# The opening of a chunk-attention and channel-mix kernel in another written order, with the diagonal blocks on the scalar engine

## The chip, the cores and the metric

The kernel runs on one core of a Trainium2 chip. The metric is the device time of one execution, in microseconds. The engines of the core work side by side, each through a queue of its own in the order in which the program was written: TensorE (PE) multiplies, VectorE (DVE) and ScalarE (ACT) do arithmetic on tiles, GpSimd (POOL) does what little is left to it, and SyncE (SP) issues the DMA transfers. One engine waits for another by semaphores.

## The reference

```python
# q, k, v: (8, 8, 576, 64): batch, heads, tokens, head width; chunks of 64 tokens
scores = matmul(q_chunk, k_chunk.T) / sqrt(64)
attn = exp(scores - max(scores)); attn = attn / (sum(attn) + 1e-9)
x = matmul(attn, v_chunk)                       # heads side by side: (8, 576, 512)

x_prev = x shifted by one token, zero at the start of each batch entry
xk = mu_k * x + (1 - mu_k) * x_prev             # mu_k, mu_r: 512 numbers each
xr = mu_r * x + (1 - mu_r) * x_prev
k = relu(xk @ w_k)                              # 512 -> 1024, w_k in float64
out = sigmoid(xr @ w_r) * ((k * k) @ w_v)       # w_r 512 x 512, w_v 1024 x 512
```

The weights arrive as 8-byte floats and are read as pairs of 32-bit words. Each is turned into a high and a low part on the chip, and each product with a weight is made of three passes: high by high, high by low, low by high.

## The kernel before

The 4608 tokens are cut into 36 tiles of 128 and 18 groups of two tiles (numbers 0 to 17). For each tile t the steps have these names, with a step number behind the point:

- `nq`, `nk`: load q and k of tiles 0 to 5 as they lie (L162); `bq`, `bk`: load q and k of a whole group, from group 3 on, as 32 x 32 blocks, 16 or 32 DMAs each (L200); `v`: load v, four DMAs (L179).
- `T`: turn q and k of a tile, for tiles 0 to 5 by PE with copies to `qT` and `kT`, later by DVE. `S`: scores (S.0 on PE), maximum, subtraction, exponential on ACT (S.3), sum, division. `P`: P.0 turns the probabilities on PE, P.1 copies them, P.2 multiplies them with v on PE (`xps`), P.4 copies the result to `x`.
- `Mk`, `Mr`: the two mixtures. For tiles 0 to 3 PE makes them (L520) by products with 16 diagonal blocks of 128 x 128, which hold mu and 1 - mu; for later tiles DVE does (L532). Then follow a high part (ACT) and a low part (DVE).
- `K` g fp: a quarter of the product with `w_k` for group g (24 matmuls into `pk`), relu, square, high and low part (`kk`). `R` g tl: the product with `w_r` (12 matmuls into `pr`) and the sigmoid. `V`: the product with `w_v` (`pv`, 24 matmuls a tile) and the output.
- `sw..`, `cw..`, `hw..`: load a weight piece of 1 MB (L251), four operations on its words (two on ACT, L255 and L259, two on DVE, L262 and L268), high part and low part. There are ten pieces: `wr0`, `wr1`, `wk0` to `wk3`, `wv0` to `wv3`. `mu`: load mu_k and mu_r (L213, L214). `dg`: make the diagonal blocks (L485).

The program has two stretches. `START` is an order written out by hand for everything up to the end of groups 0 and 1, in which the weights are loaded and converted; a letter behind a colon names the engine of a step (A for ACT, D for DVE, G for POOL). `GROUP` is the order for each of the groups 2 to 17: K, R and V of the group among the attention of the next group's tiles. Each engine's queue gets its instructions in the order of these words, so that an instruction that waits holds all that stands behind it on its engine. All DMAs are issued by SP, also in that order.

Some buffers tie steps together: `v` has two buffers, so a load of v for tile t waits for P.2 of tile t - 2. The diagonal blocks lie in the buffer with the tag `st`, which `wv2` and after it `wv3` use too: `wv2` can be loaded when the last product with a diagonal block has been made, and `wv3` when `wv2` has been converted. Scores and turned probabilities share one buffer in PSUM, and `pk` and the turned q and k of the opening share two.

Of the kernel before, what the change touches and what calls it, by code (L numbers as in the profile page):

```python
# [24 lines left out]


START = """
W:14 Mk0.0:D nq0.0 nk0.0 nq1.0 T0.2 T0.3:A nk1.0 swr1.0 T0.0 T1.0 T0.1:D P0.3:D S0.0 mu.0
dg.0:G swr0.0 S0.1:D T1.1:A v0.0 T1.2 S0.2:D T1.3:A S1.0 S1.1:D S0.3:A cwr1.1:A S1.2:D S0.4:D
cwr1.0:A S1.3:A S0.5:D nk2.0 nq2.0 P0.0 S1.4:D cwr0.1:A nk3.0 P0.1:A cwr1.2:D P0.2 T2.0 T2.2  # L30
Mk3.0:D cwr0.0:A S1.5:D cwr0.2:D nq3.0 P1.0 swk2.0 T2.1:A P0.4:A T3.2 v1.0 cwr0.3:D Mr0.0
P1.1:A T2.3:A T3.3:A S2.0 cwr1.3:D Mr0.1:A T3.0 Mk0.1 nq4.0 P1.3:D nk4.0 S2.1:D S2.2:D hwr1.0:A
T3.1:A nk5.0 S3.0 hwr1.1:D S2.3:A S3.1:D S3.2:D Mk0.2:A P1.2 Mr0.2:D P1.4:A T4.2 T4.0 T4.3:A
swk0.0 hwr0.0:A v2.0 S2.4:D cwk2.0:A Mk0.3:D T5.2 nq5.0 Mr1.0 S2.5:D hwr0.1:D swk1.0 T4.1:A
Mr1.1:A cwk2.1:A P2.3:D Mr1.2:D cwk0.1:A Mk1.1 cwk2.2:D P2.0 S3.3:A T5.0 Mk1.2:A S3.4:D Mk1.3:D
P2.1:A cwk0.0:A bk3.0 R00.0 P2.2 cwk2.3:D R01.0 R00.1:A swk3.0 P2.4:A bq3.0 hwk2.0:D Mk2.0:D
swv0.0 hwk2.1:D T5.3:A Mr2.0 cwk0.2:D cwk1.0:A cwk0.3:D cwk1.1:A S3.5:D hwk0.0:A K02.0 cwk1.2:D
P3.0 hwk0.1:D R01.1:A cwk1.3:D T5.1:A hwk1.0:D P3.1:A hwk1.1:D cwk3.0:A Mk2.1 S4.0 cwk3.1:A
cwk3.2:D K02.1:A Mr2.1:A cwk3.3:D cwv0.1:A hwk3.0:A v3.0 S4.1:D K00.0 K00.1:A swv1.0 v4.0
Mr2.2:D K00.2:A K01.0 P3.2 hwk3.1:D bq4.0 S4.2:D P3.3:D cwv0.0:A S5.0 K00.3:D P3.4:A K03.0  # L40
cwv0.2:D Mk2.2:D Mk2.3:D Mk3.1 K02.2:A K02.3:D Mk3.2:D Mr3.0 cwv1.0:A S4.3:A Mk3.3:D S4.4:D
K01.1:A K01.2:A Mr3.1:A cwv0.3:D hwv0.0:A K03.1:A P4.3:D cwv1.1:A Mr3.2:D swv2.0 S5.1:D S5.2:D
cwv2.1:A K01.3:D hwv0.1:D R10.0 cwv2.0:A S4.5:D K10.0 K11.0 cwv1.2:D cwv2.2:D cwv2.3:D hwv2.0:D
S5.3:A hwv2.1:D P4.0 P4.1:A K10.1:A cwv1.3:D R11.0 R10.1:A S5.4:D K03.2:A R11.1:A hwv1.0:A
K12.0 P4.2 K03.3:D K10.2:A v5.0 V001.0 V001.1 P4.4:A hwv1.1:D swv3.0 Mk4.0:D V001.2 K10.3:D
Mk4.1:D K11.1:A cwv3.0:A K13.0 V001.3 cwv3.1:A V001.4 cwv3.2:D cwv3.3:D S5.5:D K11.2:A K12.1:A
T6.0:D Mk4.2:A P5.0 hwv3.0:A Mk1.0:D P5.1:A V001.5 v6.0 hwv3.1:D K11.3:D Mr4.0:D V001.6 V001.7
V001.8:D P5.3:D P5.2 K13.1:A V11.0 V11.1 K12.2:A P5.4:A K12.3:D V001.9:D Mk5.0:D V11.2 Mk4.3:D
V10.0 V10.1 T6.1:D Mk5.1:D T7.0:D V11.3 K13.2:A Mr4.1:A K13.3:D Mk5.2:D V11.4 V11.5 Mr4.2:D
V10.2 V10.3 Mr5.0:D V10.4 Mk5.3:D V11.6 T7.1:D V10.5 Mr5.1:D V11.7 V10.6 V10.7 Mr5.2:D V11.8:D  # L50
V10.8:D bk4.0 v7.0
"""
# [26 lines left out]
def tile_chunk_attention_channel_mix(  # L79
# [147 lines left out]
    def convert(nm, src, a, n, dst, ring):  # L230

        st = f"{ring}:{nm}"

        def words():
            return T[st].rearrange("p a (n w) -> p a n w", w=2)  # L240
# [4 lines left out]
        def high():
            return words()[:, :, :, 1]

        def f_load(_):
# [2 lines left out]
            nc.sync.dma_start(out=T[st], in_=src)  # L251
# [4 lines left out]

        def f_a(_):
            x = low().bitcast(U32)
            nc.scalar.activation(low(), x, AF.Copy, scale=0.875 * 2.0**-29, bias=0.5)  # L259

        def f_s(_):
            nc.vector.scalar_tensor_tensor(  # L262
                out=low(), in0=high(), scalar=3, in1=low(),
                op0=ALU.logical_shift_left, op1=ALU.bitwise_or,
            )
# [10 lines left out]
        def f_lo(e):
            engine[e].tensor_tensor(dst(1), low().bitcast(F32), dst(0).bitcast(F32), ALU.subtract)  # L277
# [196 lines left out]
    def make_diag():  # L474
        do.task = "dg"

        def fn(_):
            T["diag"] = tmp.tile([P, 4, NB, P], F32, tag="st", name="diag", bufs=1)
            for i, (nm, mu) in enumerate((("k", muk), ("r", mur))):
                rest = const.tile([P, NB], F32, name=f"rest{nm}")  # L480
                nc.gpsimd.tensor_scalar(rest, mu, -1.0, 1.0, ALU.mult, ALU.add)
                for n, col in enumerate((mu, rest)):
                    to = diag[nm, n] = T["diag"][:, 2 * i + n]
                    for cb in range(NB):
                        nc.gpsimd.tensor_scalar(  # L485
                            to[:, cb], ident, col[:, cb : cb + 1], None, ALU.mult
                        )
# [75 lines left out]
    def moe_k(g, fp):  # L563
        def f_mm(_):
            pk = T[f"pk{g}{fp}"] = ps_k.tile([P, 2, G], F32, tag="k", name=f"pk_{g}_{fp}")
            xk = T[f"xk{g}"]
            for e in range(2):
                f = 2 * fp + e
                n = 0
                for cb in range(NB):  # L570
                    for a, b in PASSES:
                        nc.tensor.matmul(  # L572
                            pk[:, e, :],
                            wk[a][:, cb, f * P : (f + 1) * P],
                            xk[b][:, cb, :],
                            start=(n == 0),
                            stop=(n == 3 * NB - 1),
                        )
                        n += 1

        def f_relu(e):
            r = T[f"r{g}{fp}"] = mo.tile([P, 2, G], F32, tag="relu", name=f"relu_{g}_{fp}")
            pk = T[f"pk{g}{fp}"]
            if e == "D":
                nc.vector.scalar_tensor_tensor(
                    out=r, in0=pk, scalar=0.0, in1=pk, op0=ALU.max, op1=ALU.mult
                )
                return
            nc.scalar.activation(r, pk, AF.Relu)  # L589
            nc.scalar.activation(r, r, AF.Square)  # L590
# [192 lines left out]
```

## Time and profile before

| what | value |
| --- | --- |
| median of 3 runs (lowest, highest) | 642.67 us (638.86, 645.74) |
| profiled execution, its own time | 639.14 us |
| its span from the first to the last instruction | 637.4 us |
| PE busy | 610.6 us, 96% |
| DVE busy, ACT busy, POOL busy | 400.0, 330.0, 14.7 us |
| mean granted clock of PE | 0.976 |
| DMA | 49.17 MB, mean 77 GB/s |

Busy shares are means over the span. The table of 40 slices (15.9 us each) tells the stages apart: slices 1 to 8 hold START, the rest the regular groups and the last group. In a view by time, a row begins with its start and its length; a number in brackets at its end is how long the engine stood idle before it and what ended that.

### The profile page before, as it was taken

What the parts mean: (1) busy time and instruction counts of PE and PEld (TensorE: products, weight loads), DVE (VectorE), ACT (ScalarE), POOL (GpSimd) and SP (SyncE); (2) the same over time, 40 slices, a digit from 0 to 9 for tenths busy, and PEclk for the clock granted to TensorE, in tenths of its full rate; (3) what the DMA queues carried; (4) which work ended last, traced back from release to release, by engine and by line L of the source; (5) the groups of instructions that cost most, each with busy time, mean ns of one, the idle gap of its engine ahead of it and who ended that gap; (6) DMA issues with size and microseconds to landing.
All of it is one profiled execution on the core that took longest, in us unless ns stands there. A gap on an engine that the chain in (4) does not pass through costs nothing.

```text
span 637.4 us, 14033 instructions
## 1 busy us (share of the span) xinstructions
PE 610.6 (96%) x5676; PEld 535.7 (84%) x5676; DVE 400.0 (63%) x859; ACT 330.0 (52%) x504; POOL 14.7 (2%) x24
## 2 busy tenths in 40 slices
PE   6779799989999999999999999999999999999997
PEld 5768787877989898979797979797979797979895
...
PEclk9789699997999999999999999999999999999999
...
GB/s 220 187 200 172 123 94 83 97 37 78 67 54 65 75 83 54 80 55 81 54 65 54 79 75 67 55 70 72 76 54 64 71 86 67 35 34 34 14 21 33
DMA packets 195072, 49.17 MB, mean 77 GB/s; under 512 B 186817, under 2 KB 186817, under 8 KB 195009
## 3 DMA queue, kind: packets, MB, share of 16 engines
...
q14 instruction: 20, 0.16, 0.1%
...
## 4 chain that ended last, share of the span: by engine, by line
PE 79%; SPq 8%; DMA 7%; POOL 2%; DVE 1%; issue 1%; ACT 1%; POOLq 0%; DVEq 0%; ACTq 0%
PE pv L647 30%; PE pk L572 27%; PE pr L617 14%; SPq L200 6%; DMA wv_st<-in_moe_w_v 3%; PE xps L435 3%; PE s L360 2%; DMA wk_st<-in_moe_w_k 2%; PE pt L417 2%; POOL diag L485 2%; SPq L162 1%; DMA muk<-in_moe_mu_k 1%; DMA k<-in_k 1%; SPq L179 1%; DVE wv_st L262 0%
## 5 line engine op out<-in xcount | busy, mean ns | idle before, releaser
L572 PE MATMUL pk<-xkhi,wk 128*128 128x256 f32 x1152 | 218.5, 286 | 1.6 <-ACT relu L589 1.6
L647 PE MATMUL pv<-wv,kk 128*128 128x512 f32 x864 | 205.4, 395 | 0.0
L647 PEld LDWEIGHTS pv<-wv,kk 128*128 128x128 f32 x864 | 161.6, 187 | 39.7 <-DVE wv L277 0.4
L572 PEld LDWEIGHTS pk<-xkhi,wk 128*128 128x128 f32 x1152 | 182.1, 190 | 4.0 <-ACT relu L589 2.0
L572 PE MATMUL pk<-xklo,wk 128*128 128x256 f32 x576 | 162.9, 283 | 0.0
L572 PEld LDWEIGHTS pk<-xklo,wk 128*128 128x128 f32 x576 | 109.7, 191 | 0.8
L589 ACT ACTIVATE relu<-pk 128x512 f32<-128x512 f32 x72 | 42.6, 592 | 106.3 <-PE pk L572 105.2
L617 PE MATMUL pr<-wr,xrhi 128*128 128x512 f32 x288 | 96.2, 415 | 0.0
L602 DVE TENSOR_TENSOR kk<-relu,kk 128x512 fp32r<-128x512 f32 x72 | 49.4, 687 | 68.3 <-ACT kk L131 68.3
L617 PEld LDWEIGHTS pr<-wr,xrhi 128*128 128x128 f32 x288 | 53.1, 194 | 11.7
L617 PE MATMUL pr<-wr,xrlo 128*128 128x512 f32 x144 | 58.1, 403 | 0.0
L370 DVE TENSOR_REDUCE m<-s 128x8 f32<-128x512 f32 x36 | 24.7, 687 | 53.0 <-PE s L360 53.0
L131 ACT ACTIVATE xrhi<-mixr 128x512 fp32r<-128x512 f32 x31 | 19.6, 632 | 55.8 <-DVE mixr L532 55.8
L131 ACT ACTIVATE xkhi<-mixk 128x512 fp32r<-128x512 f32 x31 | 19.6, 631 | 53.1 <-DVE mixk L532 53.1
L590 ACT ACTIVATE relu<-relu 128x512 f32<-128x512 f32 x72 | 45.5, 632 | 2.3
L131 ACT ACTIVATE kk<-relu 128x512 fp32r<-128x512 f32 x72 | 45.5, 632 | 2.1
L532 DVE SCALAR_TENSOR_TENSOR mixk<-d,muk,x 128x128 f32<-128x128 f32 (+1 forms) x144 | 38.5, 333 | 1.0
L532 DVE SCALAR_TENSOR_TENSOR mixr<-d,mur,x 128x128 f32<-128x128 f32 (+1 forms) x144 | 38.4, 331 | 0.0
L660 DVE TENSOR_TENSOR out<-pv,sg 128x512 f32<-128x512 f32 x36 | 24.0, 674 | 19.5 <-PE pv L647 18.6
L551 DVE TENSOR_TENSOR xrlo<-mixr,xrhi 128x512 fp32r<-128x512 f32 x32 | 22.2, 692 | 21.0 <-ACT xrhi L131 21.0
L551 DVE TENSOR_TENSOR xklo<-mixk,xkhi 128x512 fp32r<-128x512 f32 x32 | 22.1, 692 | 20.9 <-ACT xkhi L131 20.9
L435 PEld LDWEIGHTS xps<-pT,v 64*64 64x64 f32 x1152 | 21.1, 141 | 16.7 <-issue 8.9
...
## 6 DMA issues: line engine op xcount, KB each, us to landing
...
```

Of the source, the lines that this page charges most:

```text
L131: nc.scalar.activation(to, x, AF.Copy)
L200: nc.sync.dma_start(out=dst[pp : pp + 32, hp, s // 32 : (s + n) // 32, :], in_=src[b, j * HP + hp, t0 : t0 + n, dh * 32 : (dh + 1) * 32].r ...
L370: nc.vector.tensor_reduce(out=heads(m), in_=scores(), axis=AX.X, op=ALU.max)
L435: nc.tensor.matmul(T[f"xps{g}"][halves[c], 2 * j + a, tl * TT + e * CH : tl * TT + (e + 1) * CH], T[f"v{t}"][halves[j], hp, e, :], T[f"pT{ ...
L532: nc.vector.scalar_tensor_tensor(out=m[:, cb, s : s + w], in0=d[:, cb, s : s + w], scalar=mu[:, cb : cb + 1], in1=x[:, cb, c : c + w], op0 ...
L551: engine[e].tensor_tensor(lo[:, :, part], T[f"m{nm}{t}"], hi[:, :, part].bitcast(F32), ALU.subtract)
L572: nc.tensor.matmul(pk[:, e, :], wk[a][:, cb, f * P : (f + 1) * P], xk[b][:, cb, :], start=(n == 0), stop=(n == 3 * NB - 1),)
L589: nc.scalar.activation(r, pk, AF.Relu)
L590: nc.scalar.activation(r, r, AF.Square)
L602: engine[e].tensor_tensor(lo, T[f"r{g}{fp}"], hi.bitcast(F32), ALU.subtract)
L617: nc.tensor.matmul(pr, xr[a][:, cb, tl * TT : (tl + 1) * TT], wr[b][:, cb, :], start=(n == 0), stop=(n == 3 * NB - 1),)
L647: nc.tensor.matmul(T[f"pv{g}{tl}"], kk[a][:, f, tl * TT : (tl + 1) * TT], wv[b, f // 4][:, f % 4, :], start=(f == 0 and n == 0), stop=(f = ...
```

## The change

The change rewrites the order of START, puts the loads of mu into ACT's DMA queue, makes the diagonal blocks on ACT instead of POOL (the two small vectors 1 - mu on DVE), and cuts the relu step in two words, relu and square. The loader of a weight piece can now take ACT's queue as well; but no word of the new START asks it to, so all ten weight pieces are still issued by SP. The words of GROUP give the same instructions in the same order as before.

```diff
 START = """
-W:14 Mk0.0:D nq0.0 nk0.0 nq1.0 T0.2 T0.3:A nk1.0 swr1.0 T0.0 T1.0 T0.1:D P0.3:D S0.0 mu.0
-dg.0:G swr0.0 S0.1:D T1.1:A v0.0 T1.2 S0.2:D T1.3:A S1.0 S1.1:D S0.3:A cwr1.1:A S1.2:D S0.4:D
+W:14 Mk3.0:D nq0.0 nk0.0 T0.2 T0.0 T0.3:D mu.0:A T0.1:D Mk0.0:D nq1.0 P0.3:D nk1.0 T1.0 S0.0
+S0.1:D swr0.0 dg.0:A v0.0 S0.2:D nk2.0 S0.3:A T1.1:D T1.2 T1.3:A cwr0.0:A S1.0 nk3.0 cwr0.1:A
...
-Lq K0.0 Sa.0 Sb.0 Sa.12 K0.12 Sa.3 Sb.12 K0.3 Sb.3 Sa.45 Sb.45 K1 K2.0 Pa.0 K2.123 Pa.1
+Lq K0.0 Sa.0 Sb.0 Sa.12 K0.123 Sa.3 Sb.12 K0.4 Sb.3 Sa.45 Sb.45 K1 K2.0 Pa.0 K2.1234 Pa.1
...
+    def queue(e):
+        return nc.scalar if e == "A" else nc.sync
...
-            nc.sync.dma_start(out=muk, in_=mu_k.rearrange("(c p) -> p c", p=P))
+            queue(e).dma_start(out=muk, in_=mu_k.rearrange("(c p) -> p c", p=P))
...
-            nc.sync.dma_start(out=T[st], in_=src)
+            queue(e).dma_start(out=T[st], in_=src)
...
-                nc.gpsimd.tensor_scalar(rest, mu, -1.0, 1.0, ALU.mult, ALU.add)
+                nc.vector.tensor_scalar(rest, mu, -1.0, 1.0, ALU.mult, ALU.add)
...
-                        nc.gpsimd.tensor_scalar(
-                            to[:, cb], ident, col[:, cb : cb + 1], None, ALU.mult
-                        )
+                        if e == "A":
+                            nc.scalar.activation(
+                                to[:, cb], ident, AF.Copy, scale=col[:, cb : cb + 1]
+                            )
...
```

The first place is the head of ACT's queue. Before, it began with the copies of the turned q and k and the first exponential (`p_0`):

```order
L131 ACT_TABLE_LOAD
L131 ACTIVATE kT_106<-trk_0_131 128x4x128
L131 ACTIVATE qT_105<-trq_1_146 128x4x128
L131 ACTIVATE kT_106<-trk_1_204 128x4x128
L380 ACTIVATE p_0_209<-p_0_209 128x512
```

Now the same place holds the loads of mu and the 16 diagonal blocks:

```order
L216 DMA muk_99<-in_moe_mu_k 128x4x1
L217 DMA mur_100<-in_moe_mu_r 128x4x1
L489 ACT_TABLE_LOAD
L489 ACTIVATE diag_175<-ident_94,muk_99 128x128 x4
L489 ACTIVATE diag_175<-ident_94,restk_176 128x128 x4
L489 ACTIVATE diag_175<-ident_94,mur_100 128x128 x4
L489 ACTIVATE diag_175<-ident_94,restr_186 128x128 x4
L383 ACTIVATE p_0_201<-p_0_201 128x512
L131 ACTIVATE kT_106<-trk_1_208 128x4x128
```

Of the three copies, two (`kT` of tile 0 and `qT` of tile 1) have gone to DVE, the third stands behind the exponential, and the exponential stands behind the blocks.

The second place is SP's queue in the middle of START. Before, from the load of piece `wk1` on (`k_3` and `q_3` are the block loads `bk3` and `bq3`):

```order
L251 DMA wk1_st_467<-in_moe_w_k 128x4x512
L200 DMA k_3_506<-in_k 32x8x32 x16
L251 DMA wk3_st_569<-in_moe_w_k 128x4x512
L200 DMA q_3_572<-in_q 32x8x32 x16
L251 DMA wv0_st_590<-in_moe_w_v 128x2x1024
L179 DMA v_3_686<-in_v 64x4x64 x4
L251 DMA wv1_st_721<-in_moe_w_v 128x2x1024
L179 DMA v_4_723<-in_v 64x4x64 x4
L200 DMA q_4_774<-in_q 32x4x32 x32
L251 DMA wv2_st_904<-in_moe_w_v 128x2x1024
```

And now:

```order
L254 DMA wk1_st_426<-in_moe_w_k 128x4x512
L182 DMA v_2_452<-in_v 64x4x64 x4
L254 DMA wk3_st_466<-in_moe_w_k 128x4x512
L254 DMA wk2_st_485<-in_moe_w_k 128x4x512
L182 DMA v_3_608<-in_v 64x4x64 x4
L254 DMA wv1_st_693<-in_moe_w_v 128x2x1024
L254 DMA wv0_st_706<-in_moe_w_v 128x2x1024
L203 DMA q_3_747<-in_q 32x8x32 x16
L182 DMA v_4_811<-in_v 64x4x64 x4
L254 DMA wv2_st_826<-in_moe_w_v 128x2x1024
L182 DMA v_5_992<-in_v 64x4x64 x4
L203 DMA k_3_1012<-in_k 32x8x32 x16
```

`v_3` has moved ahead of both block loads of group 3, and the weights of `w_k` and two of `w_v` stand ahead of them too. `wk2`, the first of the `w_k` pieces before, is now the last.

The third place is the end of START in SP's queue. Before:

```order
L662 DMA out_0<-out_1_0_1313 128x512
L200 DMA k_4_1316<-in_k 32x4x32 x32
L179 DMA v_7_1349<-in_v 64x4x64 x4
L200 DMA q_5_1357<-in_q 32x8x32 x2
L179 DMA v_8_1618<-in_v 64x4x64 x4
```

And now:

```order
L674 DMA out_0<-out_0_0_1193 128x512
L182 DMA v_6_1215<-in_v 64x4x64 x4
L674 DMA out_0<-out_0_1_1225 128x512
L182 DMA v_7_1289<-in_v 64x4x64 x4
L203 DMA k_4_1314<-in_k 32x4x32 x32
L674 DMA out_0<-out_1_1_1348 128x512
```

`v_7` has moved from behind the 32 DMAs of `k_4` to ahead of them.

More of the change, by code (lines that the diff above doesn't have):

```diff
@@ L27 @@
 START = """
-W:14 Mk0.0:D nq0.0 nk0.0 nq1.0 T0.2 T0.3:A nk1.0 swr1.0 T0.0 T1.0 T0.1:D P0.3:D S0.0 mu.0
-dg.0:G swr0.0 S0.1:D T1.1:A v0.0 T1.2 S0.2:D T1.3:A S1.0 S1.1:D S0.3:A cwr1.1:A S1.2:D S0.4:D
[L30 to L51, printed above, removed]
+W:14 Mk3.0:D nq0.0 nk0.0 T0.2 T0.0 T0.3:D mu.0:A T0.1:D Mk0.0:D nq1.0 P0.3:D nk1.0 T1.0 S0.0
@@ new lines @@
+S0.1:D swr0.0 dg.0:A v0.0 S0.2:D nk2.0 S0.3:A T1.1:D T1.2 T1.3:A cwr0.0:A S1.0 nk3.0 cwr0.1:A
+S0.4:D S0.5:D S1.1:D T2.2 S1.2:D T2.3:A nq2.0 cwr0.2:D P0.0 cwr0.3:D P0.1:A P0.2 swr1.0 S1.3:A
+T3.2 P0.4:A nq3.0 S1.4:D S1.5:D hwr0.0:A cwr1.0:D Mr0.0 cwr1.1:A v1.0 T2.0 P1.0 swk0.0 hwr0.1:D
+nq4.0 T2.1:A P1.1:A P1.3:D cwr1.2:D Mk0.1 nk4.0 T3.3:A cwr1.3:D Mr0.1:A S2.0 T3.0 S2.1:D P1.2
+Mk0.2:A Mr0.2:D nq5.0 T3.1:A S2.2:D S3.0 P1.4:A nk5.0 T4.2 swk1.0 S3.1:D cwk0.1:A Mk0.3:D
+cwk0.0:A S3.2:D S2.3:A T4.0 T4.3:A Mk1.1 hwr1.0:A v2.0 Mr1.0 swk3.0 T4.1:A Mk1.2:A T5.2 Mr1.1:A
@@ new lines @@
+S2.4:D S2.5:D T5.3:A hwr1.1:D Mk1.3:D S3.3:A swk2.0 cwk0.2:D cwk0.3:D cwk1.1:A Mr1.2:D P2.0
+P2.1:A hwk0.0:A S3.4:D T5.0 S3.5:D P2.3:D Mk2.0:D Mk1.0:D hwk0.1:D R00.0 P2.2 R00.1:A R01.0
+P2.4:A cwk2.1:A cwk1.0:D cwk1.2:D T5.1:A P3.0 cwk1.3:D P3.1:A cwk2.0:A Mr2.0 Mr2.1:A K00.0
+hwk1.0:D v3.0 hwk1.1:D cwk2.2:D R01.1:A P3.2 cwk2.3:D cwk3.0:A S4.0 K01.0 S5.0 swv1.0 P3.3:D
+Mk2.1 swv0.0 cwk3.1:A hwk2.0:A cwk3.2:D hwk2.1:D cwk3.3:D K00.1:A K01.1:A K02.0 K00.2:A
+hwk3.0:D cwv0.0:A K01.2:A hwk3.1:D bq3.0 cwv0.1:A Mr2.2:D K03.0 P3.4:A cwv1.0:A Mk2.2:A
@@ new lines @@
+cwv0.2:D P4.3:D cwv0.3:D Mk3.1 Mk2.3:D v4.0 cwv1.1:A Mr3.0 swv2.0 Mk3.2:D Mk3.3:D S4.1:D
+K00.3:A Mr3.1:A K00.4:D hwv0.0:A Mr3.2:D K02.1:A R10.0 K10.0 K01.3:A T6.0:D K02.2:A cwv1.2:D
+K02.3:A K01.4:D cwv1.3:D R11.0 R10.1:A K03.1:A cwv2.0:A cwv2.1:A K11.0 hwv0.1:D K03.2:A K02.4:D
+R11.1:A K03.3:A S5.1:D cwv2.2:D V001.0 cwv2.3:D K10.1:A K03.4:D hwv2.0:A hwv1.0:A S4.2:D S4.3:A
+hwv2.1:D K12.0 V001.1 v5.0 hwv1.1:D V001.2 K10.2:A S5.2:D S4.4:D S5.3:A bk3.0 K11.1:A K11.2:A
+K10.3:A S4.5:D S5.4:D K10.4:D swv3.0 P4.0 P4.1:A K11.3:A S5.5:D cwv3.1:A V001.3 P4.2 cwv3.0:D
@@ L52 @@
+K11.4:D K12.1:A K13.0 K12.2:A bq4.0 P4.4:A V001.4 cwv3.2:D cwv3.3:D hwv3.0:A P5.3:D P5.0 V001.5
+T7.0:D P5.1:A K13.1:A hwv3.1:D V001.6 Mk4.0:D K12.3:A V001.7 Mk4.1:D V001.8:D Mk4.2:A P5.2 v6.0
+V10.0 P5.4:A V001.9:D V10.1 V11.0 Mk5.0:D Mr4.0:D V11.1 K13.2:A K13.3:A Mr4.1:A Mk4.3:D K12.4:D
+Mk5.1:D V10.2 V10.3 Mk5.2:A K13.4:D V11.2 V11.3 V10.4 Mr4.2:D Mk5.3:D V11.4 V10.5 V11.5 v7.0
+T6.1:D V10.6 Mr5.0:D Mr5.1:D V10.7 V11.6 Mr5.2:D V11.7 bk4.0 T7.1:D V11.8:D V10.8:D
 """
 GROUP = """
-Lq K0.0 Sa.0 Sb.0 Sa.12 K0.12 Sa.3 Sb.12 K0.3 Sb.3 Sa.45 Sb.45 K1 K2.0 Pa.0 K2.123 Pa.1
@@ L57 @@
-K3.0 Pb.0 Pb.1 K3.123 Tc R0 Pa.2 Pb.2 Pa.34 Pb.34 Lv Lk Mka R1 Mkb Mra Mrb Td V0 V1
+Lq K0.0 Sa.0 Sb.0 Sa.12 K0.123 Sa.3 Sb.12 K0.4 Sb.3 Sa.45 Sb.45 K1 K2.0 Pa.0 K2.1234 Pa.1
+K3.0 Pb.0 Pb.1 K3.1234 Tc R0 Pa.2 Pb.2 Pa.34 Pb.34 Lv Lk Mka R1 Mkb Mra Mrb Td V0 V1
 """
@@ L210, in load_mu, with fn @@
         do.task = "mu"
-        def fn(_):
-            nc.sync.dma_start(out=muk, in_=mu_k.rearrange("(c p) -> p c", p=P))
-            nc.sync.dma_start(out=mur, in_=mu_r.rearrange("(c p) -> p c", p=P))
+        def fn(e):
+            queue(e).dma_start(out=muk, in_=mu_k.rearrange("(c p) -> p c", p=P))
+            queue(e).dma_start(out=mur, in_=mu_r.rearrange("(c p) -> p c", p=P))
         do(fn, "Q")
@@ L246, in high, with f_load @@
             return words()[:, :, :, 1]
-        def f_load(_):
+        def f_load(e):
             pool_, bufs = dict(st=(tmp, 1), kk0=(mx, 2), kk1=(mx, 2)).get(ring, (wts, 1))
             T[st] = pool_.tile([P, a, 2 * n], I32, tag=ring, name=f"{nm}_st", bufs=bufs)
-            nc.sync.dma_start(out=T[st], in_=src)
+            queue(e).dma_start(out=T[st], in_=src)
         def f_y(_):
@@ L475, in make_diag, with fn @@
         do.task = "dg"
-        def fn(_):
+        def fn(e):
             T["diag"] = tmp.tile([P, 4, NB, P], F32, tag="st", name="diag", bufs=1)
@@ L484, in fn @@
                     for cb in range(NB):
-                        nc.gpsimd.tensor_scalar(
-                            to[:, cb], ident, col[:, cb : cb + 1], None, ALU.mult
-                        )
-        do(fn, "G")
+                        if e == "A":
+                            nc.scalar.activation(
+                                to[:, cb], ident, AF.Copy, scale=col[:, cb : cb + 1]
+                            )
+                        else:
+                            nc.vector.tensor_scalar(
+                                to[:, cb], ident, col[:, cb : cb + 1], None, ALU.mult
+                            )
+        do(fn, "D")
     def x_mix(t):
@@ L582, in f_relu, with f_sq @@
             r = T[f"r{g}{fp}"] = mo.tile([P, 2, G], F32, tag="relu", name=f"relu_{g}_{fp}")
-            pk = T[f"pk{g}{fp}"]
             if e == "D":
[L585 to L590, printed above, removed]
+                nc.vector.tensor_scalar(r, T[f"pk{g}{fp}"], 0.0, None, ALU.max)
+            else:
+                nc.scalar.activation(r, T[f"pk{g}{fp}"], AF.Relu)
+        def f_sq(e):
+            r = T[f"r{g}{fp}"]
+            if e == "D":
+                nc.vector.tensor_tensor(r, r, r, ALU.mult)
+            else:
+                nc.scalar.activation(r, r, AF.Square)
         def f_hi(e):
@@ L606, in moe_k @@
         do(f_relu, "A")
+        do(f_sq, "A")
         do(f_hi, "A")
```

## The prediction, made before the changed kernel had run

> **What bounds the kernel now.** I read the page's busy shares and its 40 slices first.
>
> ```profile
> PE 610.6 (96%) x5676; PEld 535.7 (84%) x5676; DVE 400.0 (63%) x859; ACT 330.0 (52%) x504; POOL 14.7 (2%) x24
> PE   6779799989999999999999999999999999999997
> PEclk9789699997999999999999999999999999999999
> GB/s 220 187 200 172 123 94 83 97 37 78 67 54 65 75 83 54 80 55 81 54 65 54 79 75 67 55 70 72 76 54 64 71 86 67 35 34 34 14 21 33
> ```
>
> PE bounds the whole, and from slice 11 on it is full at the full clock: nothing that the change touches can shorten that. In the first ten slices PE has gaps, and the clock falls there too. So I read the chain that ended last for the regular beat of a group.
>
> ```profile
> 194.24 2.84 PE pk L572 x24
> 197.07 1.09 PE s L360 x64
> 207.76 2.80 PE pr L617 x12
> 214.66 11.20 PE pv L647 x48
> 228.69 1.09 PE s L360 x64
> ```
>
> A group's scores follow the last ones after 228.69 - 197.07 = 31.62 us, all of it PE work: a K step is 2.84, an R step 2.80, the V of two tiles 11.20. Every gain must come from before that beat sets in. PE's timeline shows where the beat is broken first.
>
> ```profile
> 126.29 1.16 PE L360 MATMUL s<-kT,qT 64*64 64x64 f32 x64
> 143.80 0.44 PE L435 MATMUL xps<-pT,v 64*64 64x64 f32 x2 [3.30 <-DMA v<-in_v]
> 165.37 1.16 PE L360 MATMUL s<-kT,qT 64*64 64x64 f32 x64
> ```
>
> Group 2 started at 126.29 - 2.84 = 123.45 and took 165.37 - 126.29 = 39.08 us, 7.46 more than the beat. START took the rest, 123.45 us.
>
> **The change part by part.** Four losses of before should go, two new waits come. First the **wait for v of tile 7** in group 2, just shown: 3.30 us of idleness at its first load, and matmuls at a lowered clock behind it. So a wait costs its idleness and up to 4 us of lowered clock behind it. SP's timeline says why v was late.
>
> ```profile
> 124.78 16.46 SPq L200 DMA_DIRECT2D k<-in_k  x32
> 141.34 2.58 SPq L179 DMA_DIRECT2D v<-in_v  x4
> ```
>
> The 32 DMAs of k for group 4 take 16.46 us to issue, and v of tile 7 stood behind them. Now v stands ahead, so the loss of 7.46 goes. What is late next is that k: DVE turns it in the middle of group 2.
>
> ```profile
> 140.16 0.71 DVE L336 STREAM_TRANSPOSE qT<-q 128x512 f32<-128x512 f32 x1
> ```
>
> DVE needs it 140.16 - 123.45 = 16.7 us into the group. Its issue now begins after the stores of group 0 and two loads of v (2 x 2.58). Those stores come when V of group 1 (11.20) is still to do, so the issue begins some 6 us before group 2 and ends 16.5 later, 10.5 into it: 6 us of room. If that cover were gone, DVE would hold the mixtures of the next tiles behind it.
>
> Second, the **wait for v of tile 3** in START.
>
> ```profile
> 62.02 0.27 PE L572 MATMUL pk<-xkhi,wk 128*128 128x256 f32 x1
> 65.33 1.84 PE L435 MATMUL xps<-pT,v 64*64 64x64 f32 x32 [3.03 <-DMA v<-in_v]
> 69.02 1.13 PE L360 MATMUL s<-kT,qT 64*64 64x64 f32 x32 [1.86 <-DVE p L376]
> 75.36 1.95 PE L520 MATMUL mxk<-x,diag 128*128 128x128 f32 x16
> ```
>
> On SP's side of it:
>
> ```profile
> 38.69 9.32 SPq L200 DMA_DIRECT2D k<-in_k  x16
> 48.60 10.49 SPq L200 DMA_DIRECT2D q<-in_q  x16
> 59.68 2.58 SPq L179 DMA_DIRECT2D v<-in_v  x4
> ```
>
> From 62.29 to 75.36 lie 13.07 us with one `xps` and one scores step (1.09 for two tiles, so 0.55 each) and one K step: 3.94 of work, 9.1 lost. The load was issued at 59.68, behind 9.32 + 10.49 us of block loads. Now both stand behind it, and the 9.1 goes as far as nothing else holds PE there.
>
> Third, **POOL's diagonal blocks**.
>
> ```profile
> 23.15 0.63 PE L520 MATMUL mxr<-x,diag 128*128 128x128 f32 x2
> 24.89 2.23 PE L520 MATMUL mxr<-x,diag 128*128 128x128 f32 x14 [1.11 <-POOL diag L485]
> 27.05 0.69 PE L360 MATMUL s<-kT,qT 64*64 64x64 f32 x32
> ```
>
> The first mixture took 27.05 - 23.15 = 3.90 us; at full rate a mixture is 1.78 (75.36 to 77.14, the next mixture's start). 2.1 goes, since ACT has the blocks done by 14 (below).
>
> Fourth, a **load of `wk0` in ACT's way**.
>
> ```profile
> 37.32 0.60 PE L417 MATMUL pt<-ident,p 128*128 128x128 f32 x4
> 40.36 0.63 PE L315 MATMUL trq<-ident,qn 128*128 128x128 f32 x4 [2.44 <-ACT p L380]
> 45.27 0.69 PE L435 MATMUL xps<-pT,v 64*64 64x64 f32 x32
> 38.64 1.10 ACT L259 ACTIVATE wk_st<-wk_st 128x1024 int32<-128x1024 uint32 x1 [1.28 <-DMA wk_st<-in_moe_w_k]
> ```
>
> ACT stood before `wk0` until 38.64 with the exponential behind it, and PE waited. From 37.32 to 45.27 are 7.95 us for two turnings (0.43 each) and one R (2.80): 4.3 lost. Now `wk0` is issued ahead of tiles 4 and 5, so this wait goes.
>
> Of the new waits, the first is **ACT's blocks ahead of the first exponential**. DVE makes 1 - mu behind the first maximum, so 12 of the 16 blocks come after that.
>
> ```profile
> 9.75 0.69 DVE L370 TENSOR_REDUCE m<-s 128x8 f32<-128x512 f32 x1 [0.85 <-PE s L360]
> 11.21 0.63 ACT L380 ACTIVATE p<-p 128x512 f32<-128x512 f32 x1 [0.30 <-DVE p L376]
> ```
>
> For a block's price I read the groups by shape:
>
> ```profile
> L131 ACT ACTIVATE x<-xps 128x256 f32<-128x256 f32 x8 | 2.6, 394 | 0.0
> L131 ACT ACTIVATE wr<-wr_st 128x1024 fp32r<-128x1024 f32 x2 | 2.3, 1130 | 0.0
> L131 ACT ACTIVATE kT<-trk 128x512 f32<-128x512 f32 x6 | 3.5, 596 | 6.6 <-PE trk L315 6.6
> ```
>
> No row has 128 elements on ACT. Above, it is no dearer than 256 (394 ns); below, the slope from 512 to 1024 alone gives (1130 - 596)/4 = 134. Twelve take 1.6 to 4.7 us; I take 0.25 each, 3.0, since 256 is the nearest row and copies overlap a little. The exponential then starts near 10.4 + 0.4 + 3.0 = 13.8, not 11.21; behind it on ACT stand the copy of the turned k of tile 1 and the first weight steps, and DVE's sum and PE's second scores wait. DVE now does that sum at once, before tile 1's maximum, which gives 1 us back: **1.5** lost, between 0 and 3.
>
> The Trainium skill ("ScalarE: Activation LUTs", What ACT_TABLE_LOAD costs) gives 186 ns plus 0.833 a column, 93 more for a scale read per partition, and 93 of overlap. By it 512 columns are 613, as the 596 above agrees, but a block is an estimated 293 ns, and the loss would be 2.0 instead of 1.5.
>
> The second new wait is **`wk2` on ACT**. Its first step stands on ACT ahead of `wk1`'s second, of tile 5's turned q and of P.1 of tile 3; so DVE's part of `wk1`, the second K step, P.2 of tile 3 and the scores of tile 5 wait. From `wk2`'s landing to that K step there are two ACT steps and four on DVE.
>
> ```profile
> L262 DVE SCALAR_TENSOR_TENSOR wk_st<-wk_st 128x1024 int32<-128x1024 int32 x4 | 4.9, 1226 | 3.5 <-ACT wk_st L259 3.5
> L133 DVE CAST wk<-wk_st 128x1024 fp32r<-128x1024 f32 x2 | 1.4, 694 | 0.1
> ```
>
> How fast the pieces can come shows in a stretch of 4 us (the last two columns are the share of the DMA engines and GB/s):
>
> ```profile
> 32.00:36.00 4.00, 3.19 (x30) 2.99 (x29) 3.93 (x8) 3.43 (x5) 0.00 (x0) 1.00 0.97 287
> ```
>
> From landing to K step these are 2 x 1.1 (the 1130 above) + 3 x 1.2 + 0.7 = 6.5 us. Up to `wk2` there are 10.2 MB to load (two wr and four wk pieces, q and k of six tiles, v of three). At the 200 GB/s of the slices that is 51 us, at the 287 of a full stretch 36. I take 44.5, the middle, because the block loads that kept the queue half empty are behind. The K step can then start at 51. PE would be there at 50: the first K step of before started at 45.27 + 0.55 + 2.80 + 1.78 = 50.4; take off 2.1 and 4.3, add 1.5 and one turning (0.4), and it starts at 45.9, and the second comes 2.84 + 1.1 later. I take **2.0** for the wait of 1 us and the lowered clock behind it; its ends are 0 and 11.5 (landing at 51, 7.5 of wait and 4 of clock).
>
> For the loads of mu the chain of waits has one row.
>
> ```profile
> 5.60 6.92 DMA muk<-in_moe_mu_k
> ```
>
> Issued behind q, k and a weight piece, mu took 6.92 us. At the head of an empty queue it is issued near 1 and, if it took as long, lands at 8, ahead of the maximum at 9.75 behind which the blocks wait; I take nothing. Its other end is 3 us: DMA completions are counted on semaphores in turn, so the loads of k of tile 1 and of `wr0` now wait for mu, and would be issued at 8 instead of 5. The split of relu gives the same instructions. The steps moved from ACT to DVE (0.69 each) lie beside other work; without that cover they cost those 1.4 us.
>
> **The sum.** 7.5 + 9.1 + 2.1 + 4.3 - 1.5 - 2.0 = 19.5 us off the profiled execution's 639.14 (a span of 637.4 and 1.7 around it): 619.6. The median before is 3.5 above that execution, so the median of the new kernel may lie as much above; I name **620**.
>
> **The rivals.**
> - *The wait moves to `wk2`.* If weights land at the slices' average, the second K step starts at 57.5, and the 2.0 becomes 11.5: 629. For it speaks that 200 GB/s held for 32 us; against it the 287.
> - *`wv3` comes too late for V.* Its buffer holds the diagonal blocks and then `wv2`. From the last mixture to V's seventh step go two loads and two conversions, one behind the other. Before, these took from 83.68 to 108.37:
>
> ```profile
> 83.68 0.39 SPq L251 DMA_DIRECT2D wv_st<-in_moe_w_v  x1
> 107.23 1.23 DVE L277 TENSOR_TENSOR wv<-wv_st,wv 128x1024 fp32r<-128x1024 f32 x1
> ```
>
>   That is 24.7 us; PE has 2 R, 4 K, six V steps of two tiles (8.4) and 1.4 of attention in between, 26.8. With 5 us more of queueing on ACT and DVE, 2.9 stand on PE, and about as much again is lost at the lowered clock: 625.
> - *Bytes bind, and the order only permutes them.* Then START stays as long as it was, and only the wait in group 2 goes: 631.6. For it speak the first three slices; against it that the rate falls to 123 and 94 GB/s in slices 5 and 6, while PE waits for v.
> - *More goes than I counted.* If `wk2` lands at 38 and PE's small early gaps close too, the 2.0 becomes 0 and some 6 more go: 612.
> - *Slower.* SP's queue falls behind for good: a group with 32 + 32 block DMAs needs 2 x 16.46 of issue, more than the beat of 31.62, and v stands behind them as v of tile 7 did. Each recurrence costs 7.46; from the third on the gain is gone, and with three it is 642, with four 649. Against it: in before only group 2 shows it, and the regular groups' order is the same.
> - *A weight piece through ACT's queue* isn't in the changed program: ACT issues two DMAs only, those of mu. That part does nothing, at no price.
>
> **How the numbers follow.** My case 0.48 (its own range 614 to 625), `wk2` 0.13, `wv3` 0.10, bytes 0.16, more 0.08, slower 0.05. The range of 609 to 634 leaves out the slower case, about half of the bytes' one (which with the two new waits of 3.5 and the median's 3.5 comes to 638) and the edge of the better one. About 1% (6.4 us) is what a measurement of this kernel can tell from no change, as its three runs lie 1% apart. Faster by over 1% is all below 636: four cases and half of the bytes' one, 0.87. Slower by over 1% takes four recurrences and more, 0.03; within 1% keep the other half and three recurrences, 0.10.
>
> **What would show it.** Right: group 2's scores to group 3's are 31.6 apart; no wait of `xps` for v over 1 us; the first mixture at full rate before 23; group 2 starting near 111. Wrong: ACT idle before a `wk_st` step for more than 4 us at 44; `pv` waiting for `wv`; DVE's turning in group 2 waiting for k; the DMA share near one up to 60 with START no shorter.

## The result, and the profile after

The changed kernel takes 617.93 us (median of 4 runs, 617.13 to 620.49), the kernel before 640.83 (4 runs, 638.86 to 645.74): a ratio of 0.9639, 95% interval 0.9572 to 0.9705. It is faster by 22.9 us; 620 was forecast. The profiled execution of the changed kernel took 620.49 us with a span of 618.7, 18.65 less than the 639.14 of before. The medians differ by 4 us more than these two executions, because the profiled one of before is near the fastest of its kernel and that of the changed kernel is its slowest.

The page of the changed kernel, busy shares and two rows of its 40 slices:

```profile
PE 601.6 (97%) x5676; PEld 529.2 (86%) x5676; DVE 399.8 (65%) x860; ACT 332.5 (54%) x519; POOL 0.7 (0%) x6
PE   5888999999999999999999999999999999999997
PEclk9798999999999999999999999999999999999999
```

PE and its clock are now full from slice 5 on; before, PE dipped in slices 5 and 9 too, and the clock in slices 5 and 10. What is left of gaps lies in the first four slices, 62 us. PE's timeline of the changed kernel gives the marks of the opening:

```profile
47.52 0.37 PE L580 MATMUL pk<-xkhi,wk 128*128 128x256 f32 x1
50.73 0.69 PE L438 MATMUL xps<-pT,v 64*64 64x64 f32 x32
53.01 0.39 PE L580 MATMUL pk<-xkhi,wk 128*128 128x256 f32 x1 [1.12 <-DVE wk L133]
115.10 1.16 PE L363 MATMUL s<-kT,qT 64*64 64x64 f32 x64
128.59 1.16 PE L438 MATMUL xps<-pT,v 64*64 64x64 f32 x64
146.72 1.16 PE L363 MATMUL s<-kT,qT 64*64 64x64 f32 x64
```

Three marks matter from here on: the first K step (47.52, before 50.49), the scores of group 2 (115.10, before 126.29), and those of group 3 (146.72, that is 31.62 later, before 39.08). `xps` with v of tile 3 (50.73) and with v of tile 7 (128.59) wait for nothing. The rest of the program has not moved: from the scores of group 2 to the end of the span are 618.7 - 115.10 = 503.6 us, and before 637.4 - 126.29 = 511.1, which is 503.6 and the 7.5 of the wait in group 2. So the gain of the profiled execution is 11.2 us of the opening and 7.5 of group 2.

SP's timeline, from the weight pieces on:

```profile
42.45 1.59 SPq L254 DMA_DIRECT2D wv_st<-in_moe_w_v  x2
44.09 15.27 SPq L203 DMA_DIRECT2D q<-in_q  x16
70.50 0.39 SPq L254 DMA_DIRECT2D wv_st<-in_moe_w_v  x1
73.58 9.34 SPq L203 DMA_DIRECT2D k<-in_k  x16
83.01 0.40 SPq L254 DMA_DIRECT2D wv_st<-in_moe_w_v  x1
```

Before, the first two pieces of `w_v` went out at 59.13 and 62.31, the third at 83.68 and the fourth at 95.67; now at 42.45, 70.50 and 83.01. The blocks take no less time to issue than before (15.27 and 9.34 us for 16 each, against 10.49 and 9.32), but the pieces that PE needs sooner stand ahead of them. Not all of these 15.27 us are issuing. The trace shows eight semaphores that count the landings of the DMAs, used in turn, so each issue waits until the DMA eight issues earlier has landed. For 6.2 of the 15.27 us SP stood before pieces of `w_k` and `w_v` that had not landed yet. So a large piece also holds back the small loads that follow it.

ACT's timeline shows the new work and two waits for weight pieces:

```profile
3.46 1.28 ACT L489 ACT_TABLE_LOAD   x1 [3.46 <-DMA muk<-in_moe_mu_k]
10.29 1.28 ACT L489 ACTIVATE diag<-ident,restk 128x128 f32<-128x128 f32 x4 [4.27 <-DVE restk L484]
13.82 0.61 ACT L383 ACTIVATE p<-p 128x512 f32<-128x512 f32 x1
40.19 1.11 ACT L262 ACTIVATE wk_st<-wk_st 128x1024 int32<-128x1024 uint32 x1 [2.39 <-DMA wk_st<-in_moe_w_k]
47.53 1.14 ACT L262 ACTIVATE wk_st<-wk_st 128x1024 int32<-128x1024 uint32 x1 [2.30 <-DMA wk_st<-in_moe_w_k]
```

mu landed at 3.46, the first exponential came at 13.82 (before 11.21), `wk1` landed at 40.19 and `wk2` at 47.53.

### The profile page after: what moved, and what is told of

Same layout as the page of the kernel before. It is cut to its first block, busy times and chain, and to the rows that moved or that the text cites. A ratio compares the mean times of both kernels' runs of the same rounds, so it can differ in the third digit from the quotient of the medians.

```text
span 618.7 us, 14035 instructions
## 1 busy us (share of the span) xinstructions
PE 601.6 (97%) x5676; PEld 529.2 (86%) x5676; DVE 399.8 (65%) x860; ACT 332.5 (54%) x519; POOL 0.7 (0%) x6
## 4 chain that ended last, share of the span: by engine, by line
PE 91%; DMA 4%; SPq 3%; DVE 1%; issue 0%; ACT 0%; DVEq 0%
PE pk L580 33%; PE pv L659 33%; PE pr L629 16%; PE xps L438 3%; PE s L363 3%; DMA wk_st<-in_moe_w_k 3%; PE pt L420 2%; SPq L165 2%; SPq L182 1%; DMA wr_st<-in_moe_w_r 1%; PE mxk L528 1%; PE mxr L528 0%; SPq L254 0%; DVE wk_st L265 0%; DVE wk L280 0%
## 5 line engine op out<-in xcount | busy, mean ns | idle before, releaser
L629 PE MATMUL pr<-wr,xrhi 128*128 128x512 f32 x288 | 93.7, 406 | 0.0
L629 PEld LDWEIGHTS pr<-wr,xrhi 128*128 128x128 f32 x288 | 51.4, 188 | 11.0
L629 PE MATMUL pr<-wr,xrlo 128*128 128x512 f32 x144 | 56.8, 395 | 0.0
L131 ACT ACTIVATE pT<-pt 128x512 f32<-128x512 f32 x36 | 21.3, 591 | 22.6 <-PE pt L420 22.6
```

The source lines that it names most:

```text
L131: nc.scalar.activation(to, x, AF.Copy)
L629: nc.tensor.matmul(pr, xr[a][:, cb, tl * TT : (tl + 1) * TT], wr[b][:, cb, :], start=(n == 0), stop=(n == 3 * NB - 1),)
```

## The experiments

Each kernel is the one before, or the changed one, with words of START moved or a few lines changed. Medians are of 4 to 10 runs; a ratio is to the kernel before, run in the same round. For the opening I read two marks in each profile: the first K step, and the scores of group 2, behind which everything takes 503.6 us where group 2 has no wait.

**v of tile 7, put ahead in the kernel before.**

```diff
-V10.8:D bk4.0 v7.0
+V10.8:D v7.0 bk4.0
```

> The kernel before, with one step moved: the load of v of tile 7 goes ahead of the block loads of k for group 4. My step: group 2's scores to group 3's fall from 39.08 to 31.6 us and the time by 7.5 us (ratio 0.988); START stays at 123.5. Rival: k of group 4 comes too late for DVE instead, and less than 4 us is won.

Measured: 631.91 us (628.43 to 636.23), ratio 0.984 (0.9786 to 0.9893). PE's timeline:

```profile
130.84 1.16 PE L360 MATMUL s<-kT,qT 64*64 64x64 f32 x64
162.46 1.16 PE L360 MATMUL s<-kT,qT 64*64 64x64 f32 x64
```

Group 2 takes 162.46 - 130.84 = 31.62 us: this one move takes the 7.46 away, and nothing of the rest of the change is needed for it. The medians differ by 10.6 and the interval reaches from 6.9 to 13.7, so the 7.46 lies within it. The profiled execution is the slowest of its four (636.23): from its first K step (51.19) to the scores of group 2 are 79.65 us, where the profile of before has 75.80 with the same order up to there. So the opening of one program varies by some 4 us.

**v of tile 7, put back in the changed kernel**, behind `bk4.0`.

> The changed kernel with v of tile 7 moved back behind the block loads of k for group 4. If the place of that load alone carries the gain in group 2: group 2 takes 39 us again, START still ends at 112.3, and the time rises by 7.5 us to about 626. If the rest of the new order matters for it, the rise is under 4 us.

Measured: 617.39 us (615.29 to 620.6), ratio 0.9615 (0.9568 to 0.9661). Group 2 stays at 31.62. SP's timeline:

```profile
105.02 16.39 SPq L203 DMA_DIRECT2D k<-in_k  x32
121.51 3.40 SPq L182 DMA_DIRECT2D v<-in_v  x4
```

Group 2's scores come at 114.02 in this run, and its first `xps` at 127.51. The 32 DMAs start 9 us ahead of the scores instead of close to them, so v is issued in time even from behind. In the changed kernel the new place of v is thus a second way to the same end; the other is that SP is earlier altogether.

**v of tile 3, put ahead of group 3's blocks in the kernel before.** This is the second term of the prediction by itself: that 9.1 us of the opening are the wait for this load.

```diff
-P2.1:A cwk0.0:A bk3.0 R00.0 ...
+P2.1:A cwk0.0:A v3.0 bk3.0 R00.0 ...
```

> The kernel before, with one step moved: the load of v of tile 3 goes ahead of the block loads of k for group 3. My prediction's step (the wait is v's): P.2 of tile 3 follows at 62.3 and up to 9.1 us go, START ends near 114.5. Rival, from a closer look at the trace: ACT stands before wv0 until 65 with a part of wk3 behind it, so the scores of tile 5 and the last K step of group 0 still start at 69 to 70, and START ends within 1.5 us of 123.5.

Measured: 641.4 us (637.41 to 643.71), ratio 0.9978 (0.9945 to 1.0012), no change. PE's timeline, then ACT's:

```profile
63.56 0.69 PE L435 MATMUL xps<-pT,v 64*64 64x64 f32 x32
72.14 1.13 PE L360 MATMUL s<-kT,qT 64*64 64x64 f32 x32 [7.88 <-DVE p L376]
```

```profile
68.12 1.10 ACT L259 ACTIVATE wv_st<-wv_st 128x1024 int32<-128x1024 uint32 x1 [6.48 <-DMA wv_st<-in_moe_w_v]
```

`xps` waits no more, but the scores behind it wait 7.88 us instead. ACT stands 6.48 us before a piece of `w_v` that is still behind the blocks in SP's queue, and what PE needs next stands behind that on ACT. The wait for v was only the first to be seen of several with one cause.

**Group 3's blocks put behind the first two pieces of `w_v` in the kernel before.**

```diff
-... bk3.0 R00.0 ... swk3.0 P2.4:A bq3.0 hwk2.0:D ... swv1.0 v4.0
+... R00.0 ... swk3.0 P2.4:A hwk2.0:D ... swv1.0 bk3.0 bq3.0 v4.0
```

> The kernel before, with both block loads of group 3 moved behind v of tile 3 and the pieces wv0 and wv1, so that v and the weights come earlier. If SP's block loads were the cause of the whole 9.1 us between 62.29 and 75.36, START ends near 114.5 and the time falls by 8 to 9 us; if only v's wait counted, by 3 to 5 us. If bytes bind, nothing changes.

Measured: 646.83 us (644.97 to 647.87), ratio 1.0071 (1.0042 to 1.0099): slower, a little. PE's, ACT's and SP's rows:

```profile
64.43 1.95 PE L520 MATMUL mxk<-x,diag 128*128 128x128 f32 x16
96.66 0.58 PE L572 MATMUL pk<-xkhi,wk 128*128 128x256 f32 x1 [16.61 <-ACT relu L589]
```

```profile
93.01 1.13 ACT L259 ACTIVATE wv_st<-wv_st 128x1024 int32<-128x1024 uint32 x1 [19.53 <-DMA wv_st<-in_moe_w_v]
```

```profile
45.35 13.85 SPq L200 DMA_DIRECT2D k<-in_k  x16
59.24 9.38 SPq L200 DMA_DIRECT2D q<-in_q  x16
71.34 16.08 SPq L200 DMA_DIRECT2D q<-in_q  x32
87.54 0.38 SPq L251 DMA_DIRECT2D wv_st<-in_moe_w_v  x1
```

The mixture that came at 75.36 in before comes at 64.43, so all of the 9 us is gone there. But the third piece of `w_v` goes out at 87.54, behind 64 block DMAs, and PE waits 16.61 us later on. Issue time on SP isn't saved by shifting the blocks; it must be shifted to where no weight is due.

**SP's order alone, in the kernel before.** The blocks stand where the changed kernel has them; mu, `wk2`, POOL's blocks and the order of PE, ACT and DVE stay as before.

```diff
-... bk3.0 R00.0 ... bq3.0 hwk2.0:D ... v4.0 ... bq4.0 S4.2:D ... v5.0 V001.0 ... swv3.0 Mk4.0:D ... bk4.0 v7.0
+... R00.0 ... hwk2.0:D ... bq3.0 v4.0 ... S4.2:D ... v5.0 bk3.0 V001.0 ... swv3.0 bq4.0 Mk4.0:D ... v7.0 bk4.0
```

> The kernel before with SP's order of transfers in the opening set as in the change (group 3's block loads of q behind wv1, of k behind v5, of q for tile 4 behind wv3, v of tile 7 ahead of k of tile 4); mu, wk2, the diagonal blocks and the order of PE, ACT and DVE stay as they were. Theory: the order of SP alone carries most of the opening's 11.1 us and group 2's 7.46: group 2 starts at or ahead of 115 and the time is 620 to 627. Rival: without the new order on PE and ACT the opening's steps wait for blocks that now come later (as in the run that moved them behind wv1 alone), group 2 starts at 118 or later, and the time is 629 to 636.

Measured: 619.05 us (617.94 to 620.29), ratio 0.9654 (0.9604 to 0.9703), as good as the whole change. Its PE timeline, and the busy times from 60 to 112 us (PE, weight loads, DVE, ACT, POOL, then the granted clock), first of this kernel and then of before:

```profile
24.74 3.07 PE L520 MATMUL mxr<-x,diag 128*128 128x128 f32 x14 [1.84 <-POOL diag L485]
50.59 0.36 PE L572 MATMUL pk<-xkhi,wk 128*128 128x256 f32 x1
114.90 1.16 PE L360 MATMUL s<-kT,qT 64*64 64x64 f32 x64
```

```profile
60.00:112.00 52.00, 52.00 (x430) 45.62 (x429) 44.34 (x83) 32.91 (x48) 0.00 (x0) 1.00 0.43 98
```

```profile
60.00:112.00 52.00, 45.44 (x380) 39.89 (x378) 34.17 (x62) 32.85 (x46) 0.00 (x0) 0.90 0.42 112
```

PE still waits for POOL at 24.74, and the first K step comes at 50.59, as late as in before. But from there PE is full and at the full clock: 64.3 us to the scores of group 2 instead of 75.8. The third and fourth piece of `w_v` go out at 70.16 and 83.07, as early as in the changed kernel.

**The reverse: SP's block loads of before in the changed kernel.** v of tile 7 stays ahead.

```diff
-... Mr1.0 swk3.0 ... swk2.0 cwk0.2:D ... bq3.0 cwv0.1:A ... swv2.0 ... bk3.0 K11.1:A ... bq4.0 P4.4:A
+... Mr1.0 bk3.0 swk3.0 ... swk2.0 bq3.0 cwk0.2:D ... cwv0.1:A ... bq4.0 swv2.0 ... K11.1:A ... P4.4:A
```

> The changed kernel with three block loads back at their places of before in SP's queue: k of group 3 ahead of wk3, q of group 3 behind wk2, q of tile group 4 ahead of wv2. PE's, ACT's and DVE's order, mu, the diagonal blocks and v of tile 7 stay as in the change. Theory: the opening's 11 us hang on SP's order: group 2 starts at 120 or later and the time is 625 to 634. Rival: the new order on PE and ACT carries part of it by itself: group 2 starts by 116 and the time stays under 622.

Measured: 632.13 us (630.72 to 633.92), ratio 0.9863 (0.9812 to 0.9913). PE's timeline:

```profile
44.89 0.36 PE L580 MATMUL pk<-xkhi,wk 128*128 128x256 f32 x1
58.34 0.45 PE L438 MATMUL xps<-pT,v 64*64 64x64 f32 x2 [10.37 <-DMA v<-in_v]
125.34 1.16 PE L363 MATMUL s<-kT,qT 64*64 64x64 f32 x64
```

PE is 5.6 us earlier than in before at the first K step, then waits 10.37 for v of tile 3 and comes to group 2's scores only 1 us earlier than before did. The third and fourth piece of `w_v` go out at 82.66 and 95.15, as late as in before. The time is that of the kernel before with v of tile 7 ahead (631.91). The new order of PE, ACT and DVE, mu and the diagonal blocks give nothing without SP's order, and little with it (619.05 against 617.93).

**`wk2` ahead of `wk3` in the changed kernel.** Both go out on SP's queue, one right behind the other (at 36.05 and 36.70 in the changed kernel). (The expectation names ACT's queue; that is a slip, no piece goes there.)

```diff
-... Mr1.0 swk3.0 T4.1:A ... swk2.0 cwk0.2:D
+... Mr1.0 swk2.0 swk3.0 T4.1:A ... cwk0.2:D
```

> The changed kernel with weight piece wk2 issued on ACT's queue ahead of the piece after it (wk3, on SP's side of the program's order) instead of behind. Theory that wk2 is the late one: it lands about 3 us earlier than 47.5, the second K step starts at 50 to 51 instead of 53.0, and the time is 615 to 617. Rival: bytes bind there, whichever comes second pushes the steps behind it, and the time stays 616 to 620.

Measured: 615.15 us (613.33 to 616.71), ratio 0.9591 (0.954 to 0.9643). ACT's and PE's rows:

```profile
45.19 1.16 ACT L262 ACTIVATE wk_st<-wk_st 128x1024 int32<-128x1024 uint32 x1
```

```profile
47.59 0.37 PE L580 MATMUL pk<-xkhi,wk 128*128 128x256 f32 x1
111.33 1.16 PE L363 MATMUL s<-kT,qT 64*64 64x64 f32 x64
```

`wk2` is there when ACT comes to it at 45.19, nothing waits behind it, and from the first K step to group 2's scores are 63.74 us with PE full, where the changed kernel needs 115.10 - 47.52 = 67.58. So the wait for `wk2` costs 3.8 us with its lowered clock in this pair of profiles; against a second profile of the changed kernel, where this stretch is 65.12 (109.94 - 44.82), it is 1.4. The median is 2.8 below the changed kernel's. The three kernels with `wk2` ahead, this one and two further down, have medians from 615.14 to 615.16; the changed kernel, run twice, and its three variants with `wk2` last and the opening's block loads in the new order have medians from 617.39 to 618.01.

**The price of ACT's blocks.** In one kernel they stand behind the first exponential and the copy behind it; in the other they are made on POOL, as before, with mu still loaded through ACT's queue.

```diff
-S0.1:D swr0.0 dg.0:A v0.0 S0.2:D nk2.0 S0.3:A T1.1:D T1.2 T1.3:A cwr0.0:A
+S0.1:D swr0.0 v0.0 S0.2:D nk2.0 S0.3:A T1.1:D T1.2 T1.3:A dg.0:A cwr0.0:A
```

> The changed kernel with ACT's 16 diagonal blocks put behind the first exponential and its copy instead of ahead of them. Theory of the prediction: the blocks ahead of the exponential cost PE about 1.5 us, so the time is 616 to 617. Rival: the first scores are early enough anyway, since PE waits for k of tile 4 at 31.5, and nothing is gained: 617 to 620. The first mixture can start no earlier than the blocks end.

```diff
-S0.1:D swr0.0 dg.0:A v0.0
+S0.1:D swr0.0 dg.0:G v0.0
```

> The changed kernel with the diagonal blocks and 1 - mu made on POOL as before, and mu still loaded through ACT's queue. By the prediction's terms: 2.1 us of waiting for POOL's blocks come back and 1.5 us of ACT's go, in all +0.6 (618 to 620). Rival: with mu landed at 3.5 instead of 6.9, POOL is done before the first mixture at 21.5, and the time is the same or 1.5 us less (616 to 618), so that the early load and not ACT's work takes the wait away.

Measured: behind the exponential 618.01 us (615.24 to 619.05), ratio 0.963 (0.9576 to 0.9684); on POOL 617.95 (617.43 to 618.38), ratio 0.9633 (0.9576 to 0.9691). Of the first, ACT's exponential and PE; of the second, POOL, PE and ACT:

```profile
10.80 0.63 ACT L383 ACTIVATE p<-p 128x512 f32<-128x512 f32 x1 [7.67 <-DVE p L379]
```

```profile
15.24 1.09 PE L318 MATMUL trk<-ident,kn 128*128 128x128 f32 x4 [2.58 <-DMA kn<-in_k]
```

```profile
10.87 2.85 POOL L494 TENSOR_SCALAR diag<-ident,restr 128x128 f32<-128x128 f32 x4
```

```profile
19.84 2.78 PE L529 MATMUL mxr<-x,diag 128*128 128x128 f32 x16
44.83 0.36 PE L581 MATMUL pk<-xkhi,wk 128*128 128x256 f32 x1
112.98 1.16 PE L363 MATMUL s<-kT,qT 64*64 64x64 f32 x64
```

```profile
45.29 1.15 ACT L262 ACTIVATE wk_st<-wk_st 128x1024 int32<-128x1024 uint32 x1 [3.56 <-DMA wk_st<-in_moe_w_k]
```

With the exponential 3 us earlier PE only waits for the next load of k instead, until 15.24. And POOL is done at 13.7, well ahead of the first mixture at 19.84: mu landing at 3.5 instead of 12.5 takes POOL's wait away in the new order, not the change of engine. Even so the time stays, since what PE gains up to the first K step (44.83) it loses behind it: 68.15 us to group 2, with ACT waiting 3.56 for `wk2`.

**Both, and the idle clock filled.** Next the changed kernel once more, then with `wk2` ahead and the blocks on POOL, then that with 14 more warm-up products where PE is idle:

```diff
-... T1.1:D T1.2 T1.3:A cwr0.0:A S1.0 nk3.0
+... T1.1:D T1.2 W:6 T1.3:A cwr0.0:A S1.0 W:8 nk3.0
```

> The changed kernel as it is, so that the next two can be set beside it on the same chip: 616 to 621.

> The changed kernel with wk2 issued by SP ahead of wk3, and the diagonal blocks and 1 - mu on POOL with mu still loaded through ACT's queue. Theory: wk2 was what swallowed the early start that POOL's blocks gave (first K step at 44.8 instead of 47.5, second still waiting); with both, group 2 starts 2 to 4 us earlier than with wk2 alone or with POOL's blocks alone, and the time is 612 to 614.5. Rival: the loads bind up to 50 us, and the early start is swallowed by the next weight piece: 615 to 616, as with wk2 alone.

> The kernel of the run before this one (wk2 ahead of wk3, blocks on POOL) with 14 more of the opening's warm-up products, 6 behind the turning of k of tile 1 and 8 behind the scores of tile 1, where PE stands idle and the granted clock of the next stretch (10 to 24 us) was 0.63. Theory: the idle time lowers the clock; filled, PE's steps from 11 to 23 us run at the full clock and group 2 starts 1 to 3 us earlier: 1 to 3 us less than that run. Rival: the loads of k set the pace there, and nothing is gained (within 1 us), or the clock falls anyway.

Measured, in this order: 618.0 us (615.34 to 619.84), ratio 0.9649 (0.9605 to 0.9692); 615.14 (614.16 to 617.05), 0.9599 (0.956 to 0.9637); 615.16 (613.19 to 616.84), 0.9598 (0.9558 to 0.9638). With `wk2` ahead, POOL's earlier blocks add nothing to the 2.8 us that it gave alone. The rival held in the time, though not for the reason it named: in the kernel with both, no weight piece is waited for behind the first K step either.

```profile
45.63 0.36 PE L581 MATMUL pk<-xkhi,wk 128*128 128x256 f32 x1
109.37 1.16 PE L363 MATMUL s<-kT,qT 64*64 64x64 f32 x64
```

These are 63.74 us, as with `wk2` alone, so only the start of the first K step is left to differ, and that moves with the loads from run to run (47.52 and 44.82 in two profiles of the changed kernel) by as much as POOL's blocks could give. The filled kernel shows the same from the other side. From 10 to 24 us, busy times, clock, DMA share and GB/s, first of the kernel with both and then of the filled one, and two rows of the filled one's PE:

```profile
10.00:24.00 14.00, 9.44 (x102) 8.68 (x103) 10.00 (x17) 7.51 (x10) 3.12 (x6) 0.63 0.80 191
```

```profile
10.00:24.00 14.00, 11.23 (x148) 10.27 (x146) 10.88 (x18) 9.38 (x13) 3.03 (x6) 1.00 0.84 195
```

```profile
18.27 2.02 PE L529 MATMUL mxr<-x,diag 128*128 128x128 f32 x16 [0.22 <-ACT x L131]
30.16 0.63 PE L318 MATMUL trk<-ident,kn 128*128 128x128 f32 x4 [1.79 <-DMA kn<-in_k]
31.17 3.47 PE L529 MATMUL mxk<-x,diag 128*128 128x128 f32 x16
```

The products do raise the clock, from 0.63 to 1.00, and the first mixture ends by 20.3 instead of 22.9 (19.17 + 3.72 in the kernel without them). But then PE only waits longer for k of tile 4, which lands at 30.16, and behind that a mixture takes 3.47 us instead of 1.95. There PE waits for the loads, and its own speed is worth nothing.

## Why the prediction was right, point by point

- **Wait for v of tile 7: right**, 7.46 forecast and 7.46 gone, shown by one move alone. In the changed kernel either of two things is enough for it. The k of group 4, named as what is late next, was waited for nowhere. But its room was 3.0 us, not 6: its issue began at 109.01, 3.25 us ahead of group 2, took 17.58, and DVE turned k at 129.58.
- **Wait for v of tile 3: near in size, wrong in cause.** 9.1 was forecast for the stretch from 62 to 75 us; PE's gaps and lowered clock from the first K step to group 2 were worth 75.8 - 64.3 = 11.5 (15.3 by the 79.65 of the other profile with the old order). But v wasn't the cause: v alone gave nothing. It was the block DMAs ahead of the pieces of `w_v` in SP's queue. The step "both stand behind it, and the 9.1 goes" held only because the new order brings the third and fourth piece 13 us forward as well; with the first two alone the loss came back as a wait of 16.61. The prediction's rider, "as far as nothing else holds PE there", was the whole matter.
- **POOL's blocks (2.1) and `wk0` in ACT's way (4.3): both waits went, and were worth less at the end.** With ACT's 1.5 and one turning taken off they should have brought the first K step 4.5 us forward; it came 3.0 earlier in the profiled execution and 5.7 in the second profile. In the profiled execution two things fell short of these terms. The first mixture waits for nothing now, but it runs from 21.53 to 24.20 at a mean clock of 0.66, so 1.2 of the 2.1 went, and the sign "at full rate before 23" did not come. And ACT's wait moved from `wk0` to `wk1`: ACT stands 2.39 us until 40.19 with the turned probabilities of tile 2 behind it, and PE waits 1.57 us for them until 41.83.
- **`wk2`: the mechanism right, its term too small.** A landing at 44.5 was taken, 47.5 measured (43.8 in the second profile); 2.0 was put down for it, and it costs 3.8 in the first profile, 1.4 in the second and 2.8 in the medians.
- **The opening's sum** came out near because these errors have opposite signs: 11.5 + 3.0 - 3.8 = 10.7, and 0.5 more since the new order leaves that much less to do between the two marks (63.7 against 64.3): 11.2, where 12.0 was forecast. That is luck, and it rests on which execution was profiled: in the second profile of the changed kernel the scores of group 2 come at 109.94, and the opening is 16.35 us shorter than in the profile of before.
- **ACT's blocks ahead of the exponential: the start was right** (13.8, measured 13.82), **the loss of 1.5 was not there**: behind the exponential they cost the same. Twelve took from 10.29 to 13.82, 0.294 us each; the 0.25 chosen from the nearest row was too low, but they began at 10.29 and not at 10.8. By the figures of the Trainium skill ("ScalarE: Activation LUTs", What ACT_TABLE_LOAD costs) a block was an estimated 293 ns, and the trace agrees.
- **mu: right that it costs nothing**, but a gain was missed: it landed 2.7 us after its issue instead of 6.9, and in the new order that alone rids PE of POOL's wait. The load of k of tile 1 and that of `wr0` do wait for mu's semaphores, as was said, but they went out at 3.97 and 5.07, since mu had landed by then; the other end of 3 us did not come.
- **Rivals.** Bytes don't bind the whole opening, since SP's order alone gives the gain with the same bytes; only ahead of the first K step did faster work give nothing. `wv3` came in time. SP's queue doesn't fall behind: all later groups kept 31.62. That no weight piece takes ACT's queue is as it was read from the program.
